# One reordering on ScalarE and a new split of 48 small sums in a fused long-convolution and cosine-gated MLP kernel on one Trainium2 core

## The chip, the cores and the metric

The kernel runs on one core of a Trainium2 chip (trn2). A core has five engines that run their own instruction streams in order and wait for each other by semaphores: PE (TensorE, matrix products), DVE (VectorE), ACT (ScalarE), POOL (GpSimd), and SP (SyncE), which here only issues DMAs. The metric is the device time of one execution in microseconds (us); less is better. Before the change it is 3781.08 us, the median of 6 runs between 3780.34 and 3785.08.

## What is computed

A long convolution per channel (as in Hyena), and an MLP with a cosine gate on its rows:

```
h_filt = (maximum(pos_emb @ w1, 0) @ w2) * exp(-0.01 * pos)    # one filter of length 12480 per channel
u      = x * v                                                 # 4 x 12480 x 128
y      = causal convolution of u with h_filt along the sequence (by FFT of length 2*S)
rows   = (x * y).reshape(49920, 128)
h      = rows @ w_in                                           # 49920 x 2048
out    = (h * cos(h)) @ w_out                                  # 49920 x 128
```

## The kernel before, in words

**The convolution** is done by two-step transforms written as small matrix products: a first and a second forward step (`f1`, `f2`; the product with the filter's transform is in `f2`), and a first and second inverse step (`i1`, `i2`). They run batch by batch, b = 0 to 3. The second inverse step works on 30 groups of `G` = 4 columns of the sequence. For each group it needs four matrices of 96 x 2 x 104 numbers, the tile `tm`. For b = 0 most of them are made on the spot by `make_group` (line 642), which calls `make_t` and that calls `turn` (line 284) once for each matrix; the group is then stored to DRAM (`td`, line 651) and later batches load it from there (line 670). Six of the 30 groups (2, 7, 12, 17, 22 and 27, `SOME`) are made earlier, beside `i1` of batch 0, by `some_groups`; those are loaded by b = 0 too.

A matrix is the sum of two scaled terms. Two forms of it exist in `turn`: ACT writes the first term into `tm` (line 291) and DVE scales and adds the second in one instruction (line 293); or ACT writes the first term into `tm` (line 291) and the second into a spare tile (line 296), and POOL adds the two (line 297). In a group of b = 0, matrices 0 and 1 take the first form and matrices 2 and 3 the second, with one spare buffer. In `some_groups` all four take the second form, with two.

**The MLP** runs over 98 tiles of up to 128 rows of four columns each (`BANK` = 512 numbers per partition), and each tile over 16 chunks of 128 hidden units. One chunk of one tile is a step. In step i:

- PE multiplies into a bank `ph` (`moe_up`, line 737). Four banks exist, and the transposes of a tile (`moe_turn`, `moe_back`, line 126) take theirs from the same four.
- ACT scales and shifts `ph` into `a` (line 740), DVE finds the whole turns `k` (line 743), POOL subtracts them, `f` (line 746).
- One step later (`moe_act`) ACT takes the Sin of `f` (`cs`, line 751) and DVE multiplies by `ph` to the gate `gt` (line 753), which frees that bank `ph`.
- `LAG` = 4 steps later PE multiplies `gt` into the accumulator of the tile (`moe_down`, line 762). After a tile's last chunk ACT copies the sums out (`moe_evict`, `ot`, line 768), and they are transposed back and stored later.

The accumulator has one bank (`ps_acc`, tile `acc`), so that the first `moe_down` of a tile waits for the `ot` of the tile before. Once the last convolution group has been issued, every other tile takes a bank of the convolutions instead (`cv` in place of `acc` on line 762).

**The order** is written by hand (`manual_schedule`): what the Python loop issues first stands first in each engine's queue. The loop over `steps` at the end issues `moe_up` of step i, `moe_act` of step i - 1, `moe_down` of step i - 4 and, after a tile's last chunk, `moe_evict`. In the same step as `moe_evict`, `moe_turn` of a later tile follows (PE transposes and the ACT copy `at`, line 731). Then the loop draws convolution work: each `yield` of the generators gives its cost in steps, and work is drawn until what is owed is paid. A group of `i2` with b = 0 costs 3.5 steps in four parts. In part p the generator issues the p-th matrix of the next group (`units`, the iterator `early`), the products of the current group in parts 0 and 2, and between them `inverse_units` draws the loading and multiplying of the next batch's input (`u_units`: `xt`, line 392, and the sums `slots` of line 398), in which the first half of every other multiplication is on POOL and all others on DVE.

Of the kernel before, what the change touches and what calls it, by code (L numbers as in the profile page):

```python
# [9 lines left out]
F32 = mybir.dt.float32  # L10
# [20 lines left out]
def kernel(  # L31
# [51 lines left out]
    N1, N2 = 96, 120  # L83
    R = S // N2
# [15 lines left out]
    G = BANK // D  # L100
# [204 lines left out]
    def make_t(t, n2, **how):  # L305


        i = 1 if n2 < H - 1 else 0
        turn(t, rows[:, i:i + 2, :], rows[:, i + 1:i + 3, :], tw_t[:, 0, n2:n2 + 1],
             tw_t[:, 1, n2:n2 + 1], **how)  # L310
# [54 lines left out]
    def n2s(g):  # L365

        a = g * UA
        return [*range(a, a + UA), *range(N2 - UA - a, N2 - a)]
# [270 lines left out]
            yield from units(CB, I1_STEPS, lambda j: None, mm,  # L639
                             lambda j, ps: i1_evict(pool, ps, j), 2)  # L640

    def make_group(pool, g, t, summed, bufs=1):

        for i, n2 in enumerate(n2s(g)):
            if i < G - summed:
                make_t(t[:, i, :, :], n2)
            else:
                spare = pool.tile([N1, 2, R], F32, name="spare", bufs=bufs)
                make_t(t[:, i, :, :], n2, spare=spare[:, :, :])
            yield  # L650
        nc.sync.dma_start(td[g, :, :, :, :], t[:, :, :, :])

    def some_groups(pool):
        for g in SOME:
            t = pool.tile([N1, G, 2, R], F32, name="some", bufs=2)
            yield from make_group(pool, g, t, G, bufs=2)
        next(backs[0])

    def i2_units(bank, b, bufs):

        with tc.tile_pool(name="back", bufs=2, side="left" if b else "right") as pool:
            ts, xss = {}, {}

            def before(j):
                ts[j] = pool.tile([N1, G, 2, R], F32, name="tm", bufs=bufs)
                xss[j] = pool.tile([R, 2, UA * D], F32, name="xs", bufs=bufs)
                load_pairs(xss[j], x, b, n2s(j)[0], n2s(j)[UA])
                if b == 0 and j not in SOME:
                    return make_group(pool, j, ts[j], G // 2)
                nc.sync.dma_start(ts[j][:, :, :, :], td[j, :, :, :, :])  # L670

            def mm(j, ps, i):
                if i == 0:
                    ps = bank()
                i2_mm(ps, ts[j], j, i)
                return ps

            yield from units(NG, I2_STEPS, before, mm,
                             lambda j, ps: i2_out(pool, ps, xss.pop(j), b, j),
                             4 if b == 0 else 2, ahead=bufs - 1)  # L680
# [34 lines left out]
    def rows_of(n):  # L715
        return first_row(n + 1) - first_row(n)
# [7 lines left out]
    def moe_turn(pool, n):  # L724
        m = rows_of(n)
        zb = zbs.pop(n)
        pt = ps_h.tile([P, BANK], F32, name="ph")
        for i in range(G):
            transpose(pt[:, i * m:(i + 1) * m], zb[0:m, i, :], ident)
        at = pool.tile([D, BANK], F32, name="at")  # L730
        nc.scalar.copy(out=at[:, 0:G * m], in_=pt[:, 0:G * m])
        ats[n] = at

    def moe_up(pool, n, c):
        m = G * rows_of(n)
        ph = ps_h.tile([P, BANK], F32, name="ph")
        nc.tensor.matmul(ph[:, 0:m], w_in_sb[:, c * P:(c + 1) * P], ats[n][:, 0:m],  # L737
                         start=True, stop=True)
        a = pool.tile([P, BANK], F32, name="a", bufs=3)
        nc.scalar.activation(a[:, 0:m], ph[:, 0:m], AF.Identity,  # L740
                             bias=quarter[:, 0:1], scale=INV_TWO_PI)
        k = pool.tile([P, BANK], F32, name="k")
        nc.vector.tensor_scalar(out=k[:, 0:m], in0=a[:, 0:m], scalar1=ROUND,  # L743
                                scalar2=ROUND, op0=ALU.add, op1=ALU.subtract)
        f = pool.tile([P, BANK], F32, name="f")
        nc.gpsimd.tensor_tensor(f[:, 0:m], a[:, 0:m], k[:, 0:m], op=ALU.subtract)  # L746
        return ph, f, m

    def moe_act(pool, ph, f, m):
        cs = pool.tile([P, BANK], F32, name="cs")  # L750
        nc.scalar.activation(cs[:, 0:m], f[:, 0:m], AF.Sin, scale=TWO_PI)  # L751
        gt = pool.tile([P, BANK], F32, name="gt", bufs=4)
        nc.vector.tensor_tensor(gt[:, 0:m], ph[:, 0:m], cs[:, 0:m], op=ALU.mult)  # L753
        return gt

    def moe_down(n, c, gt):
        if c == 0:

            accs[n] = bank() if made[0] == B * NG and n % 2 else \
                ps_acc.tile([P, BANK], F32, name="acc")  # L760
        m = G * rows_of(n)
        nc.tensor.matmul(accs[n][:, 0:m], w_out_sb[:, c, :], gt[:, 0:m],  # L762
                         start=(c == 0), stop=(c == NFC - 1))

    def moe_evict(pool, n):
        m = G * rows_of(n)
        ot = pool.tile([D, BANK], F32, name="ot", bufs=1)
        nc.scalar.copy(out=ot[:, 0:m], in_=accs.pop(n)[:, 0:m])  # L768
        return ot

    def moe_back(pool, n, ot):
        m = rows_of(n)
        pt = ps_h.tile([P, BANK], F32, name="ph")
        for i in range(G):
            transpose(pt[0:m, i * D:(i + 1) * D], ot[:, i * m:(i + 1) * m], ident)
        ob = pool.tile([P, 2, UA * D], F32, name="ob", bufs=1)
        nc.scalar.copy(out=ob[0:m, :, :].rearrange("p h n -> p (h n)"), in_=pt[0:m, :])
        return ob

    def moe_store(n, ob):  # L780
        row = first_row(n)
        while row < first_row(n + 1):
            b, g, n1 = row // R // NG, row // R % NG, row % R
            count = min(R - n1, first_row(n + 1) - row)
            first, _, second, _ = n2s(g)
            start = out[b * S + n1 * N2 + first, :]
            at = row - first_row(n)
            nc.sync.dma_start(
                bass.AP(tensor=start.tensor, offset=start.offset,
                        ap=[[N2 * D, count], [(second - first) * D, 2], [1, UA * D]]),  # L790
                ob[at:at + count, :, :])
            row += count

    with tc.manual_schedule():
        with tc.tile_pool(name="psum", bufs=8, space=PSUM) as psum, \
# [103 lines left out]
            nc.vector.memset(quarter[:, :], 0.25)  # L899
            nc.sync.dma_start(w_in_sb[:, :], wind[:, :])  # L900
            beside(i1_units(bank), [(w_out_sb[:, c, :], w) for c, w in out_pieces], some_groups)

        ps_acc = ctx.enter_context(tc.tile_pool(name="ps_acc", bufs=1, space=PSUM))
        ps_h = ctx.enter_context(tc.tile_pool(name="ps_h", bufs=4, space=PSUM))
        ps_c = ctx.enter_context(tc.tile_pool(name="ps_c", bufs=3, space=PSUM))
        mpool = ctx.enter_context(tc.tile_pool(name="moe", bufs=2))
# [14 lines left out]
        def load(n):  # L921
            while made[0] * R < first_row(n + 1):
                next(conv)
            moe_load(mpool, n)
# [4 lines left out]
        steps = [(n, c) for n in range(NALL) for c in range(NFC)]  # L929
        hidden, gates, ots, obs = {}, {}, {}, {}  # L930
        for i in range(len(steps) + LAG):
            if i < len(steps):
                n, c = steps[i]
                if n == 0 and c == NFC // 2:
                    load(1)
                if c == NFC - 4 and n + 2 < NALL:
                    load(n + 2)
                hidden[i] = moe_up(mpool, n, c)
            if 0 <= i - 1 < len(steps):
                gates[i - 1] = moe_act(mpool, *hidden.pop(i - 1))  # L940
            if i >= LAG:
                pn, pc = steps[i - LAG]
                moe_down(pn, pc, gates.pop(i - LAG))
                if pc == NFC - 1:
                    ots[pn] = moe_evict(mpool, pn)
            if i < len(steps):

                if c == (LAG - 1 if n else NFC - 2) and n + 1 < NALL:
                    moe_turn(mpool, n + 1)
                if c == NFC // 2 and n - 1 in ots:  # L950
                    obs[n - 1] = moe_back(mpool, n - 1, ots.pop(n - 1))
                if c == NFC // 2 + 2 and n - 1 in obs:
                    moe_store(n - 1, obs.pop(n - 1))
            owed += 1.0
            while owed > 0.0:
                owed -= next(conv, owed)
# [30 lines left out]
```

## Time and profile before

One execution was profiled. Its time was 3780.34 us; its span, from the first to the last instruction, is 3778.6 us.

| what | busy us (share of the span) | instructions |
|---|---|---|
| PE | 3699.7 (98%) | 13546 |
| DVE | 2761.6 (73%) | 5562 |
| POOL | 2591.5 (69%) | 2342 |
| ACT | 2519.0 (67%) | 4683 |
| time of the profiled execution | 3780.34 | |
| median of the 6 runs | 3781.08 | |

Stretches of the span: up to 337 us the filter, the tables and the transforms of batch 0; 337 to 580 us `i2` of batch 0, with the first MLP tiles beside it; 580 to 3000 us the other batches beside the MLP; from 3000 us the MLP alone.

How to read the views: a group line gives the source line, engine, operation, output <- inputs, how often, busy us and mean ns. A line of the view of waits reads "engine line <- releaser: us in total, times, longest us". A line of the timeline gives start, duration, engine, line, operation and tiles, "x2" where two neighbours are merged; a product of 512 columns in float32 is two matmul records, which start 0.43 us apart and are recorded as 0.59 us each, because they are pipelined. PEld is the loading of a product's stationary operand, and an idle time of 0.24 us before one is the usual spacing. In brackets stands the idle time before the instruction and what ended it.

### The profile page before, as it was taken

How to read it: one execution, taken by the hardware profiler on the slowest of the kernel's cores; microseconds unless marked ns; L12 is line 12 of the kernel's file. 1: busy time of each engine (PE TensorE's matmuls, PEld its weight loads, DVE VectorE, ACT ScalarE, POOL GpSimd, SP SyncE). 2: the span in 40 equal slices, each digit the busy share in tenths (PEclk: the TensorE clock that was granted, in tenths of full speed). 3: DMA queues.
4: the chain of work that ended last, by engine and by line, in shares of the span. 5: the costliest groups of instructions: out<-in, count | busy, mean ns of one | idle time of the engine just before them, and what ended most of it. 6: DMA issues, size and time to landing. Idle time of an engine off the chain costs nothing.

```text
span 3778.6 us, 47199 instructions
## 1 busy us (share of the span) xinstructions
PE 3699.7 (98%) x13546; PEld 2107.4 (56%) x13546; DVE 2761.6 (73%) x5562; ACT 2519.0 (67%) x4683; POOL 2591.5 (69%) x2342
## 2 busy tenths in 40 slices
PE   8898999999999999999999999999999999999999
PEld 6777555655466555555565556555566544444444
DVE  7887887688766777778766786788765566666666
ACT  5757776766665557766655567666664677777777
POOL 7667886588854665688745664788644577777776
PEclk9999999999999999999999999999999999999999
DMA  6263441022202650122103540122105200000000
GB/s 166 67 181 108 149 148 54 19 72 77 74 18 69 182 155 27 35 76 79 57 18 111 176 123 21 48 79 75 41 12 169 86 22 18 17 21 19 17 22 13
DMA packets 209498, 276.14 MB, mean 73 GB/s; under 512 B 17111, under 2 KB 146535, under 8 KB 209111
## 3 DMA queue, kind: packets, MB, share of 16 engines
q1 hardware_dynamic: 209239, 273.12, 24.3%
q8 instruction: 109, 1.79, 0.2%
q14 instruction: 150, 1.23, 0.1%
HBM read 193.64 MB, written 79.42 MB: 72 GB/s over the span
## 4 chain that ended last, share of the span: by engine, by line
PE 85%; POOL 6%; DVE 3%; ACT 2%; DMA 2%; issue 2%; SPq 0%; POOLq 0%; DVEq 0%; ACTq 0%
PE ph L737 32%; PE acc L762 27%; PE cv L762 5%; PE cv L501 5%; PE cv L476 4%; POOL f L746 3%; PE cv L404 3%; PE cv L445 3%; PE ph L126 2%; PE ps L445 1%; PE ps L404 1%; PE ps L476 1%; DVE k L743 1%; POOL tm L297 1%; ACT cs L751 1%
## 5 line engine op out<-in xcount | busy, mean ns | idle before, releaser
L746 POOL TENSOR_TENSOR f<-a,k 128x512 f32<-128x512 f32 (+1 forms) x1568 | 1985.5, 1266 | 1049.7 <-DVE k L743 1048.7
L737 PE MATMUL ph<-at,w_in_sb 128*128 128x512 f32 (+1 forms) x3136 | 1598.9, 591 | 6.0 <-DVE gt L753 5.4
L740 ACT ACTIVATE a<-ph,quarter 128x512 f32<-128x512 f32 (+1 forms) x1568 | 1072.5, 684 | 758.8 <-PE ph L737 749.0
L762 PE MATMUL acc<-gt,w_out_sb 128*128 128x512 f32 (+1 forms) x2688 | 1374.3, 593 | 9.4 <-ACT ot L768 9.1
L753 DVE TENSOR_TENSOR gt<-ph,cs 128x512 f32<-128x512 f32 (+1 forms) x1568 | 1076.9, 687 | 317.2 <-ACT cs L751 289.1
L743 DVE TENSOR_SCALAR k<-a 128x512 f32<-128x512 f32 (+1 forms) x1568 | 768.7, 490 | 620.6 <-ACT a L740 604.0
L751 ACT ACTIVATE cs<-f 128x512 f32<-128x512 f32 (+1 forms) x1568 | 980.5, 625 | 328.9 <-POOL f L746 326.6
L762 PEld LDWEIGHTS acc<-gt,w_out_sb 128*128 128x128 f32 x2688 | 505.6, 189 | 662.2 <-issue 619.3
L737 PEld LDWEIGHTS ph<-at,w_in_sb 128*128 128x128 f32 x3136 | 553.6, 190 | 338.6 <-issue 269.1
L471 POOL TENSOR_TENSOR slots<-slots,t 120x256 f32<-120x256 f32 x384 | 311.5, 817 | 58.8 <-DVE t L464 36.2
L501 PEld LDWEIGHTS cv<-slots,tm 96*104 96x104 f32 x1920 | 239.9, 170 | 108.4 <-issue 80.9
L501 PE MATMUL cv<-slots,tm 96*104 96x128 f32 x1920 | 253.5, 274 | 9.7 <-DVE tm L293 4.9
L762 PE MATMUL cv<-gt,w_out_sb 128*128 128x512 f32 (+1 forms) x448 | 224.5, 583 | 0.7 <-DVE gt L753 0.7
L476 PEld LDWEIGHTS cv<-cs,slots 120*96 120x96 f32 x1536 | 176.7, 167 | 67.6 <-issue 65.7
L476 PE MATMUL cv<-cs,slots 120*96 120x120 f32 x1536 | 183.1, 266 | 0.0
L445 PE MATMUL cv<-slots,w 124*120 124x256 f32 x576 | 173.0, 380 | 0.0
L445 PEld LDWEIGHTS cv<-slots,w 124*120 124x120 f32 x576 | 103.6, 184 | 123.8 <-issue 110.9
L404 PEld LDWEIGHTS cv<-c,slots 104*124 104x124 f32 x768 | 132.5, 192 | 71.2 <-issue 58.3
L404 PE MATMUL cv<-c,slots 104*124 104x192 f32 x768 | 151.2, 326 | 4.7 <-DVE gt L753 3.4
L762 PEld LDWEIGHTS cv<-gt,w_out_sb 128*128 128x128 f32 x448 | 84.9, 190 | 104.5 <-issue 99.5
L392 DVE TENSOR_TENSOR xt<-xt,vt 104x256 f32<-104x256 f32 x177 | 137.8, 786 | 0.0
L486 DVE TENSOR_TENSOR slots<-cv,other 96x240 f32<-96x240 f32 x384 | 133.7, 394 | 4.2 <-ACT other L484 4.2
(129 smaller groups left out, 2567.0 us busy)
## 6 DMA issues: line engine op xcount, KB each, us to landing
h<-hd SPq DMA_DIRECT2D x144, 240.0 KB
tm<-td SPq DMA_DIRECT2D x96, 312.0 KB
xt<-in_x_dram SPq DMA_DIRECT2D x120, 208.0 KB
vt<-in_v_dram SPq DMA_DIRECT2D x120, 208.0 KB
xs<-in_x_dram SPq DMA_DIRECT2D x120, 208.0 KB
zd<-zs SPq DMA_DIRECT2D x119, 208.0 KB
zb<-zd SPq DMA_DIRECT2D x96, 256.0 KB
w<-wd SPq DMA_DIRECT2D x144, 116.2 KB
```

Of the source, the lines that this page charges most:

```text
L404: nc.tensor.matmul(ps[0:KE, i * 2 * N1:(i + 1) * 2 * N1], u[:, b, 0:KE, i], c1[0:u.shape[0], :, :].rearrange("p r k -> p (r k)"), start=Tr ...
L445: nc.tensor.matmul(pi, w[:, i, :], parts[0:KE, :, k], start=True, stop=True)
L471: nc.gpsimd.tensor_tensor(y[:, r], y[:, r], t[:, r], op=op)
L476: nc.tensor.matmul(ps[0:N1, (i * 2 + r) * N2:(i * 2 + r + 1) * N2], parts[0:N2, r, :, b, i], cs[:, r, :], start=True, stop=True)
L501: nc.tensor.matmul(ps[0:R, i * D:(i + 1) * D], t[:, i, r, :], slots[0:N1, :, place, :], start=(r == 0), stop=(r == 1))
L737: nc.tensor.matmul(ph[:, 0:m], w_in_sb[:, c * P:(c + 1) * P], ats[n][:, 0:m], start=True, stop=True)
L740: nc.scalar.activation(a[:, 0:m], ph[:, 0:m], AF.Identity, bias=quarter[:, 0:1], scale=INV_TWO_PI)
L743: nc.vector.tensor_scalar(out=k[:, 0:m], in0=a[:, 0:m], scalar1=ROUND, scalar2=ROUND, op0=ALU.add, op1=ALU.subtract)
L746: nc.gpsimd.tensor_tensor(f[:, 0:m], a[:, 0:m], k[:, 0:m], op=ALU.subtract)
L751: nc.scalar.activation(cs[:, 0:m], f[:, 0:m], AF.Sin, scale=TWO_PI)
L753: nc.vector.tensor_tensor(gt[:, 0:m], ph[:, 0:m], cs[:, 0:m], op=ALU.mult)
L762: nc.tensor.matmul(accs[n][:, 0:m], w_out_sb[:, c, :], gt[:, 0:m], start=(c == 0), stop=(c == NFC - 1))
```

## The change

Two edits. In the groups of b = 0, DVE now makes matrices 0 and 2 and POOL matrices 1 and 3, and the spare tile has two buffers. `some_groups` still gives all four to POOL, with two buffers. In the loop over steps, `moe_down` of step i - 4 and the `moe_evict` behind it are issued ahead of `moe_act` of step i - 1. Since PE has no instruction in `moe_act` and ACT and DVE have none in `moe_down`, this changes the order of one engine alone: on ACT, once a tile, the copy `ot` stands ahead of the Sin of step i - 1 in place of behind it.

```diff
-    def make_group(pool, g, t, summed, bufs=1):
+    def make_group(pool, g, t, summed):
 
         for i, n2 in enumerate(n2s(g)):
-            if i < G - summed:
+            if summed < G and i % 2 == 0:
                 make_t(t[:, i, :, :], n2)
             else:
-                spare = pool.tile([N1, 2, R], F32, name="spare", bufs=bufs)
+                spare = pool.tile([N1, 2, R], F32, name="spare", bufs=2)
                 make_t(t[:, i, :, :], n2, spare=spare[:, :, :])
             yield
         nc.sync.dma_start(td[g, :, :, :, :], t[:, :, :, :])
...
-            yield from make_group(pool, g, t, G, bufs=2)
+            yield from make_group(pool, g, t, G)
...
                 hidden[i] = moe_up(mpool, n, c)
-            if 0 <= i - 1 < len(steps):
-                gates[i - 1] = moe_act(mpool, *hidden.pop(i - 1))
             if i >= LAG:
                 pn, pc = steps[i - LAG]
                 moe_down(pn, pc, gates.pop(i - LAG))
                 if pc == NFC - 1:
                     ots[pn] = moe_evict(mpool, pn)
+            if 0 <= i - 1 < len(steps):
+                gates[i - 1] = moe_act(mpool, *hidden.pop(i - 1))
```

## The prediction

> **What bounds the kernel now.** I read the page's busy times and its chain, then the view of waits, then stretches by window, then the timeline around the ends of tiles.
>
> ```profile
> PE 3699.7 (98%) x13546; PEld 2107.4 (56%) x13546; DVE 2761.6 (73%) x5562; ACT 2519.0 (67%) x4683; POOL 2591.5 (69%) x2342
> PE 85%; POOL 6%; DVE 3%; ACT 2%; DMA 2%; issue 2%; SPq 0%; POOLq 0%; DVEq 0%; ACTq 0%
> ```
>
> PE is the bound: 98% busy, 85% of the chain. So an edit on other engines is worth only what it takes from, or adds to, PE's waits. The waits that the edits touch:
>
> ```profile
> ACT cs L751 <- POOL f L746: 326.6, 882, 2.9
> PEld acc L762 <- ACT ot L768: 39.9, 45, 2.3
> PE acc L762 <- ACT ot L768: 9.1, 15, 1.5
> ACT spare L296 <- POOL tm L297: 7.2, 12, 0.7
> ```
>
> After a tile's end the first product of the next tile waits for `ot`, which stands on ACT behind a Sin that itself waits for `f`. The windows (PE, PEld, DVE, ACT, POOL busy, then the granted clock):
>
> ```profile
> 337.00:580.00 243.00, 231.15 (x919) 134.19 (x920) 201.97 (x337) 177.51 (x355) 203.88 (x185) 0.98 0.51 153
> 385.00:389.00 4.00, 3.49 (x11) 2.44 (x12) 3.06 (x7) 2.39 (x6) 3.13 (x3) 0.60 0.23 58
> 3000.00:3779.00 779.00, 773.35 (x1982) 355.64 (x1980) 493.57 (x881) 604.40 (x963) 553.81 (x440) 1.00 0.07 19
> ```
>
> Edit one acts only in 337 to 580 us, where POOL (84%) and DVE (83%) are nearly as full as PE (95%).
>
> **Edit two, `ot` ahead of the Sin.** A tile's end in the middle stretch, between two steps:
>
> ```profile
> 1629.04 1.02 PE L762 MATMUL acc<-gt,w_out_sb 128*128 128x512 f32 x2
> ...
> 1629.51 1.28 POOL L746 TENSOR_TENSOR f<-a,k 128x512 f32<-128x512 f32 x1
> ...
> 1630.77 1.02 PE L737 MATMUL ph<-at,w_in_sb 128*128 128x512 f32 x2
> 1630.82 0.63 ACT L751 ACTIVATE cs<-f 128x512 f32<-128x512 f32 x1 [0.90 <-POOL f L746]
> ...
> 1631.36 0.57 ACT L768 COPY ot<-acc 128x512 f32<-128x512 f32 x1
> ...
> 1631.98 1.12 PE L762 MATMUL acc<-gt,w_out_sb 128*128 128x512 f32 x2 [0.18 <-ACT ot L768]
> ...
> 1632.94 1.02 PE L737 MATMUL ph<-at,w_in_sb 128*128 128x512 f32 x2
> ```
>
> The last sums are ready at 1630.06 (1629.04 + 1.02), ACT is idle until `f` ends at 1630.79, and `ot` starts at 1631.36. PE's product should start at 1630.77 + 2 x 0.43 = 1631.63; it starts at 1631.98, 0.35 late, and its second half 0.10 later still (the next product is 0.96 behind it in place of 0.86): 0.45 us lost. Afterwards `ot` runs from about 1630.11 to 1630.68, inside ACT's idle time: the loss goes, and the Sin isn't late. The idle column alone understates this (0.18 here), as a record lasts 0.59 and its successor could start after 0.43. So I added up, from the start times at all 98 ends, start minus the natural start, and the 0.10. From 600 to 3000 us that gives 10.05 us at 26 tiles: 0.52 at 617, 2.73 at six tiles from 841 to 1043, 2.21 at seven from 1565 to 1766, 2.14 at six from 2418 to 2585, 1.73 at 2687 and 0.72 at five others. With `ot` at the end of the last product or of the preceding `a`, whichever is later, plus 0.05, every one of them is gone.
>
> What is behind the moved copy on ACT: this Sin, `at`, conversions of convolution banks, the next `a`. Where the Sin was ready it becomes 0.44 to 0.75 us late (0.46 from the start of `ot` to the next instruction, plus ACT's wait for the last product). Its `gt` is late with it, and late next is the `moe_up` two steps on, which takes the bank that this `gt` frees. With the Sin's new time I redid that wait for each tile: 0.80 us come back, at 1407, 1565, 2687 and in traces at four others. The convolution's banks hide the rest: 0.87 us (2262) to 1.3 us are left there before the next use, above 0.75. `td` stores, PE's and SP's queues keep their order. I take 10.05 - 0.80 = 9.25, less 0.75 for waits that return a few steps later: 8.5. Bounds: 4, the idle row alone (9.1, of which 4.2 lie before 580 and 0.8 at 584), and 10.
>
> The end, from 3000 us, has nothing to win (accumulators alternate), and the least cover:
>
> ```profile
> 3414.85 1.02 PE L762 MATMUL acc<-gt,w_out_sb 128*128 128x512 f32 x2
> ...
> 3415.93 0.63 ACT L751 ACTIVATE cs<-f 128x512 f32<-128x512 f32 x1 [0.19 <-POOL f L746]
> ...
> 3416.47 0.57 ACT L768 COPY ot<-acc 128x512 f32<-128x512 f32 x1
> ...
> 3416.60 0.69 DVE L753 TENSOR_TENSOR gt<-ph,cs 128x512 f32<-128x512 f32 x1 [0.33 <-ACT cs L751]
> ...
> 3417.44 0.19 PEld L737 LDWEIGHTS ph<-at,w_in_sb 128*128 128x128 f32 x1 [0.24 <-DVE gt L753]
> ```
>
> `ot` will start at 3415.91 (3414.85 + 1.02 + 0.04), the Sin at 3416.37, 0.44 late; `gt` ends at 3417.73 in place of 3417.29, and the load can start 0.05 later, 3417.78, 0.34 late. Over the trace, loads that start up to 0.32 us after the preceding product cost nothing, and from 0.43 on the excess plus 0.10. So 0.02 us a tile x 27 = 0.6. If the Sin were 0.75 late as elsewhere, the load would be 0.65 late: 0.22 + 0.10 = 0.33, x 27 = 8.8. I take 0.6, since these 27 ends are alike to 0.01 us. Bounds 0 and 8.8.
>
> In 337 to 580 us (six ends, the last at 584) the same sum gives 5.55 us gone and 1.84 back. But here `f` falls behind PE within every tile, from 2.6 us after its product to 6, and PE's stalls at the end are what lets it catch up; without them the next ends wait more for `gt`. I take half of 3.7: 1.8 (bounds 0, 3.7). Two ends there, 385 and 505, are followed by a granted clock of 0.60 and 0.57 for 4 us, 1.6 + 1.7 us of PE; with shorter stalls they may go: 1.0 (bounds 0, 3.3).
>
> The Trainium skill (TensorE: Matmul & The Clock Gate, HAM oscillation) asks for idle gaps over some 3.4 us before the clock falls; by that, shorter stalls here save none of this. No gap in front of these two is that long in the trace, so the trace differs, and the 1.0 stands by the windows.
>
> **Edit one.** 24 groups, 48 matrices each way, before and after: no work is added. Instruction order of both kernels: PE and SP the same. In half of the groups parts 1 and 2 fall in one MLP step, and POOL's order doesn't change at all; in the others its first sum moves ahead of `xt`, out of the part in which DVE multiplies. Rows from the timelines of POOL and ACT:
>
> ```profile
> 531.09 1.77 POOL L297 TENSOR_TENSOR tm<-tm,spare 96x208 f32<-96x208 f32 x1
> ```
> ```profile
> 532.89 0.47 ACT L296 ACTIVATE spare<-rows,tw_t 96x208 f32<-96x208 f32 x1 [0.74 <-POOL tm L297]
> ```
>
> The second row goes with two buffers: 7.2 us of ACT in all, and the `a` behind it comes sooner; POOL's next `f` was then late by 0.35, x 10 of the 12 such waits = 3.5. The first: POOL's first sum of a group takes 1.28 on the mean, its second 0.76, and 0.62 alone. In the changed groups it should fall to about 0.9: 0.4 x 11 = 4.4 of POOL. Against that, POOL gets `f`, a sum and `xt` (1.27 + 0.9 + 1.0) in one step of 2.2 us. Of 7.9 I take 3 on PE. Bounds: +8 (all of it), and -12 (11 groups in which `xt` of 1.1 delays `f` on the chain).
>
> The Trainium skill (Perfetto Trace Analysis, Optimizing Scalar/DVE Operations) speaks against this edit: POOL and DVE share a read port that one instruction locks, so that moving work between them may not help. The 1.77 row agrees with such a lock; by the rule alone the 3 would be 0 and the time 3770.4.
>
> **Sum:** 8.5 + 1.8 + 1.0 + 3.0 - 0.6 = 13.7 us. The profiled execution (span 3778.6, 1.7 around it) took 3780.34, 0.7 under the median; from the median, 3781.08 - 13.7 = 3767.4.
>
> **Rivals.**
> 1. *Batch 0's stretch gives all back*: POOL's rate sets it, and edit one leaves it. For: `f` lags there through each tile. Against: POOL is idle 39 of 243 us. 3781.1 - 8.5 + 0.6 = 3773.2.
> 2. *Slower: POOL's step with two extra operations.* In 337 to 580 us, `f` behind sum and `xt` delays Sin and `gt`, and PE stalls at tile ends for the bank `ph`. Price 12 as above plus four more clock drops at 1.65 = 18.6: 3773.2 + 18.6 = 3791.8. Beyond 7.9 the change is slower, beyond 15.4 by over 0.2%. For: PE waits there for `gt` 3.9 us even now. Against: the next step has no sum, and four steps of lag smooth it.
> 3. *The late Sin costs at the end* 8.8 rather than 0.6: 3767.4 + 8.2 = 3775.6. For: PE's ends are modelled. Against: `a` follows a modelled end by 0.04 throughout.
> 4. *Edit one doesn't do what it says* in half the groups is counted above.
>
> **Chances.** Forecast 0.55 (own range 3761 to 3773), rival 1 0.20, rival 2 0.11, rival 3 0.14. Within 0.2%, 7.6 us, a measurement of this kernel can't tell it from none: that is 3773.5 to 3788.6. Faster: 0.51 + half of rival 1 = 0.61. Slower: 0.10 of rival 2. Same: the rest, 0.29. Rival 3, rival 1 and the bounds of batch 0's stretch put the upper end at 3781; the lower is 3757: the forecast less the rest of the bounds (1.5 + 1.9 + 2.3 + 5 = 10.7).
>
> **What would show it.** Right: `acc` waiting for `ot` nearly gone between 600 and 3000 us; Sin later by 0.4 at tile ends after 3000 with PE's 773 us unchanged; 12 waits of `spare` gone; the stretch 337 to 580 shorter by some 6. Wrong: PE waiting for `gt` where it waited for `ot`, a longer stretch after 3000, more clock drops before 580.

## The result and the profile after

| kernel | median us (lowest to highest, runs) | ratio to before (95% interval) |
|---|---|---|
| before | 3781.97 (3779.14 to 3786.94, 36) | |
| after | 3771.77 (3769.3 to 3775.1, 16) | 0.9973 (0.9966 to 0.9979) |

The change makes the kernel 10.2 us faster. The execution that was profiled took 3775.76 us (span 3774.0), 4.0 above the median of after, and that of before 1.6 below the median of the table. So a comparison of these two traces shows 4.6 us (3778.6 - 3774.0) of the 10.2, and a difference of 2 or 3 us between two single executions proves little. Where it matters I use several kernels' traces.

The page of after, busy times and the chain's shares by engine:

```profile
PE 3695.9 (98%) x13546; PEld 2108.8 (56%) x13546; DVE 2778.6 (74%) x5562; ACT 2517.6 (67%) x4683; POOL 2569.0 (68%) x2342
PE 86%; DVE 4%; DMA 3%; POOL 3%; ACT 2%; issue 2%; SPq 0%; POOLq 0%; DVEq 0%; ACTq 0%
```

PE is the bound as before. POOL lost 22.5 us of work and DVE gained 17.0, though both do the same operations as before: each count is unchanged. The waits of the whole execution that answer to those shown of before:

```profile
ACT cs L751 <- POOL f L746: 384.1, 877, 2.9
...
PEld ph L737 <- ACT at L731: 16.7, 41, 0.8
...
ACT ot L768 <- PE acc L762: 11.4, 66, 0.3
...
PEld cv L501 <- DMA tm<-td: 10.8, 12, 3.3
```

`ot` now waits for the last sums (at most 0.3 us), as the diff intends, where before it waited behind a Sin. For 583 to 2995 us, the same view of after:

```profile
PEld acc L762 <- ACT ot L768: 5.9, 24, 0.4
...
PEld cv L501 <- DMA tm<-td: 4.9, 7, 1.3
...
PE cv L501 <- DMA tm<-td: 3.4, 4, 1.2
```

Before, the first of these lines read 31.6 us, 40 times, up to 2.3, and there was a second, of PE itself, with 4.9 us; that one is gone. What is left of the first is 24 waits of 0.25 on the mean (0.4 at most), about the usual spacing of 0.24. The two lines of `tm` grew: they were 2.9 and 2.3. The timeline at the end of a tile, the same tile as shown of before:

```profile
1629.36 1.02 PE L762 MATMUL acc<-gt,w_out_sb 128*128 128x512 f32 x2
...
1629.82 1.28 POOL L746 TENSOR_TENSOR f<-a,k 128x512 f32<-128x512 f32 x1
...
1630.42 0.58 ACT L768 COPY ot<-acc 128x512 f32<-128x512 f32 x1 [0.17 <-PE acc L762]
...
1631.10 1.02 PE L737 MATMUL ph<-at,w_in_sb 128*128 128x512 f32 x2
1631.13 0.63 ACT L751 ACTIVATE cs<-f 128x512 f32<-128x512 f32 x1
...
1631.95 1.02 PE L762 MATMUL acc<-gt,w_out_sb 128*128 128x512 f32 x2
```

`ot` starts 0.04 us after the sums (1630.38), while `f` still runs, and the Sin follows `f` (1631.10) by 0.03. The next `moe_down` starts 0.85 us after its `moe_up`, the undisturbed distance (2 x 0.43); before it was 1.21. This is what the prediction described for PE and for `ot`.

Two stretches by window (PE, PEld, DVE, ACT, POOL busy, then the granted clock), and one that follows a long wait:

```profile
337.00:583.00 246.00, 232.10 (x921) 134.09 (x922) 211.10 (x341) 176.30 (x359) 183.77 (x187) 0.98 0.51 152
...
431.00:435.00 4.00, 4.00 (x9) 1.76 (x8) 2.65 (x6) 1.92 (x4) 1.91 (x3) 0.59 0.47 138
2995.00:3774.00 779.00, 773.62 (x1984) 355.74 (x1982) 492.52 (x881) 604.95 (x963) 553.83 (x440) 1.00 0.07 19
```

In the first, before had 204.97 of DVE and 205.57 of POOL in a window of the same length: 6.1 us more and 21.8 less. The second shows that a drop of the clock remains, at another place; it follows this piece of the chain (start, us, what):

```profile
424.19 0.92 PE ph L737 x2
425.11 5.15 DMA tm<-td
430.25 0.04 issue
430.30 1.13 PE cv L501 x8
```

PE waits at 430 for the matrices of a group that is loaded, not made. To place the gains, I cut each trace at events that all kernels have: the first convolution product of batch 0's inverse, and the ends of tiles 5, 69 and 95 (in before at 337, 581, 2991 and 3728 us). Times are in us, each stretch from one trace; the ratios come from timed runs, each against before in its own session. The medians of before were 3782.0 beside after, 3784.7 beside e1 to e4, 3784.6 beside e5 to e8 and 3785.9 beside e9 and e10, so that ratios and not medians are to be compared.

| kernel | batch 0, to tile 5 | tiles 5 to 69 | tiles 69 to 95 | median | ratio (95% interval) |
|---|---|---|---|---|---|
| before | 243.7 | 2409.5 | 737.16 | | |
| after | 244.8 | 2402.8 | 736.97 | 3771.8 | 0.9973 (0.9966 to 0.9979) |
| e1 `ot` first, no turns | 242.7 | 2405.8 | 736.97 | 3774.4 | 0.9975 (0.9966 to 0.9985) |
| e2 turns only | 244.6 | 2411.3 | 737.16 | 3784.4 | 1.0000 (0.9991 to 1.0009) |
| e3 second spare only | 243.7 | 2414.6 | 737.16 | 3782.8 | 0.9999 (0.9990 to 1.0008) |
| e4 after, `tm` load first | 242.3 | 2398.4 | 736.97 | 3768.4 | 0.9963 (0.9949 to 0.9976) |
| e5 after, `moe_turn` first too | 245.0 | 2406.5 | 736.97 | 3778.9 | 0.9985 (0.9976 to 0.9994) |
| e6 `ot` and load first, no turns | 242.6 | 2399.4 | 736.97 | 3767.9 | 0.9956 (0.9943 to 0.9968) |
| e7 after, all matrices by DVE | 240.1 | 2403.5 | 736.97 | 3769.4 | 0.9957 (0.9942 to 0.9973) |
| e8 after, all by POOL | 249.5 | 2403.7 | 736.97 | 3781.7 | 0.9995 (0.9986 to 1.0004) |
| e9 e6, all by DVE | 236.4 | 2399.6 | 736.97 | 3763.9 | 0.9940 (0.9927 to 0.9954) |
| e10 e7, ACT's copies kept | 238.6 | 2405.9 | 736.97 | 3767.9 | 0.9955 (0.9941 to 0.9969) |

### The profile page after: what moved, and what is told of

It is laid out like the page before. It is cut to its first block, busy times and chain, and to the rows that moved or that the text cites. A ratio compares the mean times of both kernels' runs of the same rounds, so it can differ in the third digit from the quotient of the medians.

```text
span 3774.0 us, 47191 instructions
## 1 busy us (share of the span) xinstructions
PE 3695.9 (98%) x13546; PEld 2108.8 (56%) x13546; DVE 2778.6 (74%) x5562; ACT 2517.6 (67%) x4683; POOL 2569.0 (68%) x2342
## 4 chain that ended last, share of the span: by engine, by line
PE 86%; DVE 4%; DMA 3%; POOL 3%; ACT 2%; issue 2%; SPq 0%; POOLq 0%; DVEq 0%; ACTq 0%
PE ph L737 33%; PE acc L762 28%; PE cv L762 5%; PE cv L501 5%; PE cv L476 4%; PE cv L445 3%; PE cv L404 3%; PE ph L126 2%; POOL f L746 2%; DMA hd<-h 2%; PE ps L404 1%; DMA tm<-td 1%; PE ps L476 1%; ACT cs L751 1%; DVE gt L753 1%
## 5 line engine op out<-in xcount | busy, mean ns | idle before, releaser
L743 DVE TENSOR_SCALAR k<-a 128x512 f32<-128x512 f32 (+1 forms) x1568 | 796.4, 508 | 549.9 <-ACT a L740 537.7
```

## The experiments

**e1, e2, e3: the two edits, and the second spare buffer, each alone.** e1 is before with only this:

```diff
-            if 0 <= i - 1 < len(steps):
-                gates[i - 1] = moe_act(mpool, *hidden.pop(i - 1))
             if i >= LAG:
...
+            if 0 <= i - 1 < len(steps):
+                gates[i - 1] = moe_act(mpool, *hidden.pop(i - 1))
```

> Edit two alone: the copy of a tile's sums ahead of the Sin, the groups of batch 0 as before. Theory A (the prediction's terms): 8.5 us gained between 580 and 3000 us, 2.8 in batch 0's stretch with the clock drops, 0.6 lost after 3000: about 10.7 us faster, ratio 0.9972. Theory B (the stretch of batch 0 gives everything back, because there the vector engines and the loads set the pace): 8.5 - 0.6 = about 8 us faster, 0.9979, and 337 to 581 us as long as before. In both, no wait of acc for ot in the profile from 580 us on, and the Sin at a tile's end 0.4 to 0.75 us late.

e2 is before with the other edit, to `make_group` and its call in `some_groups`, as the change has it:

```diff
-            if i < G - summed:
+            if summed < G and i % 2 == 0:
...
-                spare = pool.tile([N1, 2, R], F32, name="spare", bufs=bufs)
+                spare = pool.tile([N1, 2, R], F32, name="spare", bufs=2)
```

> Edit one alone: matrices by DVE and POOL by turns and two spare buffers, the Sin ahead of the sums' copy as before. Theory A: POOL's sums in batch 0's stretch take about 0.77 us on the mean instead of 1.02, and 3 us of it reach PE: 3778 to 3779, ratio 0.9992. Theory B: POOL's time is saved (48.9 to some 37 us) but PE waits instead for the loads of the six groups that were made earlier, so no gain: 1.0000 plus or minus 0.0005.

e3 is before with a second buffer and no turns:

```diff
-                    return make_group(pool, j, ts[j], G // 2)
+                    return make_group(pool, j, ts[j], G // 2, bufs=2)
```

> Only the second spare buffer of edit one; matrices 0 and 1 by DVE, 2 and 3 by POOL as before, the Sin first as before. Every engine's order is that of before. Theory A: the 12 waits of ACT's spare for POOL's sum (7.2 us) go and some 2 us reach PE: 0.9995. Theory B: the waits go, and nothing reaches PE: 1.0000. If POOL's sums keep their mean of 1.02 us here, the shorter sums of the changed kernel come from the turns and not from the buffer.

Measured: 0.9975 for e1, 1.0000 for e2, 0.9999 for e3. The whole gain is that of the copy's place; the turns and the buffer bring nothing (to 0.1%). In e3 the 12 waits of `spare` for POOL's sum (7.2 us) are gone, and nothing of them reaches PE. What the turns do is seen in three groups of 337 to 583 us, first of before (the last numbers are busy us, mean ns, and the idle time ahead):

```profile
L746 POOL TENSOR_TENSOR f<-a,k 128x512 f32<-128x512 f32 x83 | 105.3, 1269 | 27.5 <-DVE k L743 27.5
...
L297 POOL TENSOR_TENSOR tm<-tm,spare 96x208 f32<-96x208 f32 x48 | 48.9, 1019 | 2.5 <-ACT spare L296 2.5
L743 DVE TENSOR_SCALAR k<-a 128x512 f32<-128x512 f32 x84 | 43.5, 517 | 21.7 <-ACT a L740 21.7
```

The same groups of after:

```profile
L746 POOL TENSOR_TENSOR f<-a,k 128x512 f32<-128x512 f32 x82 | 104.0, 1269 | 47.4 <-DVE k L743 46.4 <-PE ph L737 1.0
...
L743 DVE TENSOR_SCALAR k<-a 128x512 f32<-128x512 f32 x83 | 51.6, 622 | 10.4 <-ACT a L740 9.7 <-POOL f L746 0.7
...
L297 POOL TENSOR_TENSOR tm<-tm,spare 96x208 f32<-96x208 f32 x48 | 37.2, 774 | 1.4 <-ACT spare L296 1.2
```

POOL's sums fell from 1.019 to 0.774 us each, 11.7 us in all, more than the 4.4 forecast. But DVE's `k` rose from 0.517 to 0.622 (8.7 us over 83 of them), and `k` stands ahead of every `f`. What POOL saved in all, 21.8 us, became waiting: its idle time ahead of `f` grew by 19.9. In e3 the sums stay at 1.021, so it is the turns and not the buffer that shorten them; `k` is at 0.564 there, so that nearly half of its rise comes with the second buffer alone. My reading is that the blocked time went from a POOL operation that had some slack to a DVE operation ahead of it; that `k` passes it on to PE is not shown by itself.

**e4 and e6: the load of the matrices ahead of the load of the input.** The chain above waits for `tm<-td`. In the code that load stands on SP behind the load of `xs` (`load_pairs`), which waits until DVE's `zs` of an earlier group has read the buffer that it fills (0.8 us at this group). e4 is after with:

```diff
+                made_here = b == 0 and j not in SOME
+                if not made_here:
+                    nc.sync.dma_start(ts[j][:, :, :, :], td[j, :, :, :, :])
                 load_pairs(xss[j], x, b, n2s(j)[0], n2s(j)[UA])
-                if b == 0 and j not in SOME:
+                if made_here:
                     return make_group(pool, j, ts[j], G // 2)
-                nc.sync.dma_start(ts[j][:, :, :, :], td[j, :, :, :, :])
```

> The changed kernel, and in the second inverse step the load of a group's matrices is issued ahead of the load of x on SP's queue, so that it no longer stands behind a transfer that waits for DVE's product of two groups before. Theory B (the stretch's gain goes into these waits): PE's waits for tm from DRAM (3.8 us before 583, 3.4 later, in the profile of the changed kernel) fall below 2 us in all, and the time is 3 to 6 us under the changed kernel: about 3767, ratio to before 0.996. Theory A (they are a matter of single runs): the time is that of the changed kernel within 1.5 us, 0.9973.

e6 has the same edit and the copy's place, and matrices 0 and 1 by DVE and 2 and 3 by POOL as in before. Unlike what its expectation says, it keeps the second spare buffer, as after does.

> Edit two and the load of a group's matrices ahead of the load of x, without edit one (matrices 0 and 1 by DVE, 2 and 3 by POOL, one spare buffer). If edit one is worth nothing or costs up to 1 us, as its run alone showed: 0.9962 plus or minus 0.0006, as with it (0.9963), or 1 us better. If edit one's saving on POOL was only held back by the loads and shows once these are early: 3 us slower than with it, 0.9971.

SP's timeline at the load of the group that stalled at 430, in after:

```profile
423.47 0.33 SPq L651 DMA_DIRECT2D td<-tm  x1
424.69 0.31 SPq L373 DMA_DIRECT2D xs<-in_x_dram  x1
425.11 0.34 SPq L670 DMA_DIRECT2D tm<-td  x1
```

and in e4:

```profile
423.01 0.33 SPq L651 DMA_DIRECT2D td<-tm  x1
423.44 0.37 SPq L669 DMA_DIRECT2D tm<-td  x1
424.24 0.33 SPq L373 DMA_DIRECT2D xs<-in_x_dram  x1
```

The load starts 0.43 us after the store ahead of it, in place of 1.64. In e4 no wait of PE's products for `tm<-td` remains, in e6 1.1 us of it, where after has 3.8 (to 583 us) and 3.4 (behind that). Tiles 5 to 69 are 5.2 us shorter than without the edit (mean of e4, e6 and e9, 2399.1, against 2404.4 for after, e1, e7, e8 and e10; the two sets don't overlap). So a load came last at some places where PE no longer waited for `ot`. How much of the 5.2 us the early load would have given with the Sin first is open: no run has that. e6 against e1, both without turns (e6 with the second buffer): 0.9956 against 0.9975, whose intervals still overlap; the traces are the clearer evidence. e6 is no slower than e4 (0.9963), so that edit one's saving was not merely held back by the loads.

**e5: a later Sin still.** e5 is after with the transposes of the next tile, and so the copy `at`, also ahead of the Sin:

```diff
+            if i < len(steps):
+                if c == (LAG - 1 if n else NFC - 2) and n + 1 < NALL:
+                    moe_turn(mpool, n + 1)
             if 0 <= i - 1 < len(steps):
...
-                if c == (LAG - 1 if n else NFC - 2) and n + 1 < NALL:
-                    moe_turn(mpool, n + 1)
```

> The changed kernel with the transposes of the next tile and their copy at issued ahead of the Sin as well, so that the Sin of a tile's end is late by two copies (0.92 us) in place of one. The prediction's rule (a load of weights up to 0.32 us late costs nothing, from 0.43 on the excess plus 0.10): after 3000 us the load is 0.80 late at each of 27 ends, 0.37 + 0.10 = 0.47 a tile, 12.5 us; between 600 and 3000 us 3.2 us more than in the changed kernel; about 15.7 us slower than the changed kernel, ratio to before 1.0015. Rival (a late Sin is made up for elsewhere, the four steps of lag hide it): the time of the changed kernel, 0.9973, and the 27 tiles after 3000 us as long as before (737.2 us between the last products of tiles 69 and 95).

Measured: 0.9985, 736.97 us for tiles 69 to 95, the same as in after to 0.01 us, though the Sin is later by one more copy. A tile's end there in e5:

```profile
3385.80 0.64 ACT L751 ACTIVATE cs<-f 128x512 f32<-128x512 f32 x1
...
3386.37 0.19 PEld L737 LDWEIGHTS ph<-at,w_in_sb 128*128 128x128 f32 x1 [0.24 <-issue]
3386.47 0.69 DVE L753 TENSOR_TENSOR gt<-ph,cs 128x512 f32<-128x512 f32 x1 [1.27 <-ACT cs L751]
3386.79 1.02 PE L737 MATMUL ph<-at,w_in_sb 128*128 128x512 f32 x2
```

The load of the second `moe_up` behind the tile's end begins 0.10 us before this `gt` has even begun, and its product starts 0.37 us before `gt` ends (3387.16). It does not take the bank that this `gt` frees. In after the same load, at 3412.75, names its releaser:

```profile
3411.59 0.63 ACT L751 ACTIVATE cs<-f 128x512 f32<-128x512 f32 x1
...
3412.12 0.57 ACT L731 COPY at<-ph 128x512 f32<-128x512 f32 x1
...
3412.25 0.69 DVE L753 TENSOR_TENSOR gt<-ph,cs 128x512 f32<-128x512 f32 x1 [0.79 <-ACT cs L751]
...
3412.75 0.51 PEld L737 LDWEIGHTS ph<-at,w_in_sb 128*128 128x128 f32 x2 [0.35 <-ACT at L731]
```

It starts when the copy `at` has ended (3412.69) and before `gt` has (3412.94): it takes the bank of the transposes. In before it is the other way round. There the same load (3417.44, shown in the prediction) names `gt`, which ended at 3417.29, and it starts before `at` has ended (3417.52):

```profile
3416.93 0.59 ACT L731 COPY at<-ph 128x512 f32<-128x512 f32 x1
```

The waits behind 2995 us say the same of all tiles there, first of before, then of after:

```profile
PEld ph L737 <- DVE gt L753: 13.2, 55, 0.3
```
```profile
PEld ph L737 <- ACT at L731: 9.1, 26, 0.4
PEld ph L737 <- DVE gt L753: 7.2, 29, 0.4
```

26 of the 55 went from `gt` to `at`, one for each tile's end. The line of after with 26 waits for `at` stands in every trace with `ot` first except e5's, where `at` comes earlier; before, e2 and e3 have none. So the edit changed more than ACT's order: with the copy ahead of the Sin, the four banks `ph` are taken in another order, and the late `gt` frees the one that the third `moe_up` takes. That load has time to spare even in e5: it starts at 3388.08, 0.92 us after this `gt`. By the ratios e5 is 4.5 us slower than after (0.0012 x 3782; the intervals just overlap). Its trace doesn't say where: it is 3.7 us longer than that of after over tiles 5 to 69, in small parts without a wait that carries it, and no longer than those of e1 and e10 by more than 1 us. That stays open.

**e7, e8, e10: who makes the matrices.** e1 to e3 say that the turns win nothing; another split might. e7 is after with no matrix of batch 0's groups on POOL, e8 with all on POOL:

```diff
-            if summed < G and i % 2 == 0:
+            if i < G - summed:
...
-                    return make_group(pool, j, ts[j], G // 2)
+                    return make_group(pool, j, ts[j], 0)
```

```diff
-                    return make_group(pool, j, ts[j], G // 2)
+                    return make_group(pool, j, ts[j], G)
```

> The changed kernel with all four matrices of a group of batch 0 made by DVE, none by POOL. If POOL's rate sets the stretch of batch 0 (37 us of sums go from it): several us faster than the changed kernel, 0.9955. If DVE, or the port that both share, sets it as much as POOL: DVE gets 48 more instructions of 0.5 to 0.9 us, k behind them comes later, and the stretch of 245 us grows by 5 to 20 us: 0.999 to 1.003.

> The changed kernel with all four matrices of a group of batch 0 made by POOL, none by DVE. If DVE's rate sets the stretch: faster than the changed kernel by several us, 0.9955. If POOL's does: 48 more sums of 0.8 us and 48 more terms on ACT of 0.45 us, the stretch grows by 15 to 35 us: 1.001 to 1.006. If both this and all by DVE are slower, neither engine alone sets the stretch, and moving sums between them has nothing to win.

Measured: 0.9957 and 0.9995, and 240.1 and 249.5 us for batch 0's stretch, where after has 244.8. So the split matters after all: the intervals of e7 and e8 lie apart. `k` in e7, then in e8, in 337 to 583 us:

```profile
L743 DVE TENSOR_SCALAR k<-a 128x512 f32<-128x512 f32 x85 | 40.2, 472 | 4.7 <-ACT a L740 4.5
```
```profile
L743 DVE TENSOR_SCALAR k<-a 128x512 f32<-128x512 f32 x81 | 59.9, 740 | 13.1 <-ACT a L740 11.7 <-POOL f L746 0.7
```

With `ot` first, and the load where after has it, the stretch goes with the length of `k`: 0.472 (e7) 240.1, 0.515 (e1) 242.7, 0.622 (after) 244.8, 0.740 (e8) 249.5. POOL's sums change along with `k` in these four, so that the runs don't tell the two apart. In e7 DVE does 48 more terms and is 92% busy (226.4 of 246), and the stretch is still the shortest of these four: the busy share of DVE does not set it. In e8 PE also waits 9.1 us for POOL's sums. But e7 takes two things away, POOL's sums and 48 copies `spare` of ACT (22 us). e10 puts the copies back, into buffers that nothing reads:

```diff
                 make_t(t[:, i, :, :], n2)
+                if i % 2:
+                    spare = pool.tile([N1, 2, R], F32, name="spare", bufs=2)
+                    row = 1 if n2 < H - 1 else 0
+                    nc.scalar.activation(spare[:, :, :], rows[:, row + 1:row + 3, :], AF.Copy,
+                                         scale=tw_t[:, 1, n2:n2 + 1])
```

> e7 (all matrices of batch 0's groups by ACT and DVE) with the 48 scaled copies on ACT that POOL's sums needed still made, into two spare buffers that nothing reads. It is work added that the output doesn't use. It tells POOL's share of e7's gain from ACT's. Theory 'POOL's sums set that stretch': it stays at 240 to 241 us, 0.9957 of before. Rival 'ACT's copies set it' (22 us of ACT came off in e7): it goes back to 242.7 to 245 us, where e1 and the kernel after are, 0.9965 to 0.9975 of before.

Measured: 0.9955 and 238.6 us; `k` takes 0.477. The copies on ACT cost nothing, and e7's gain comes from POOL's sums having gone. e10's stretch is even 1.5 shorter than e7's; that difference lies where the clock stayed low for longer in e7, in 431 to 435 us (0.57, in e10 0.92).

**e9: the parts that helped, together.** e6 with no matrix of batch 0's groups on POOL.

> e6 (the sums' copy ahead of the Sin, the matrices' load ahead of that of the input) with all 96 matrices of batch 0's groups in the form of ACT and DVE, none on POOL. If the gains are of different places they add: e7's stretch of batch 0 was 240.07 us against 242.64 in e6, its later stretches those of the kernel after, and e6's later stretches 3 us shorter than that. Theory 'they add': 3767.9 - 2.6 = 3765.3 us, 0.9950 of before (0.9943 to 0.9957), stretch of batch 0 at 239 to 241 us. Rival 'both take the same waits for the matrices' (the waits of products for loaded or made matrices move from one to the other): 0.9956 as e6, stretch near 242.5 us.

Measured: 3763.89 us, 0.9940 (0.9927 to 0.9954), the fastest of all medians, 22 us under before in the same session (3785.86). Its stretch of batch 0, 236.4 us, is 6.2 shorter than e6's where 2.6 was expected. Part of this is the clock: in e6 it was 0.56 from 341 to 349 us, and the 33rd product of the stretch starts 11.6 us after the first, where in e9 (0.82) and e4 (0.92) it is 9.0. Without these 2.5 us 3.7 are left. The trace of e9 shows no drop of the clock between 345 and 3750 us, as e4 doesn't.

## Why the prediction was right, and where it was wrong

**Right: what edit two removes.** Every wait of PE for `ot` behind 583 us is gone, with `ot` where the arithmetic put it. The term of 8.5 for tiles behind 580 us: the two traces give 6.7 (2409.5 - 2402.8); the mean of the five kernels with `ot` first and the old load order against before, e2 and e3 gives 7.4 (2411.8 - 2404.4). It lay within its bounds, 4 and 10.

**Wrong: "late next is the `moe_up` two steps on, which takes the bank that this `gt` frees".** That was read rightly off the trace of before, and it holds there. The prediction took it over to after, but the edit itself changes the order of the banks: in after this load waits for `at`. So the 0.80 that was to come back, the 0.6 lost at the end and rival 3 had no path. Tiles 69 to 95 became 0.19 us shorter, not 0.6 longer, and Sin's lateness is free there even with one more copy ahead of it. As far as the prediction goes this is luck, since nothing in it foresaw the new order; what a Sin this late would cost in the old one no run shows.

**Wrong: what takes back.** The allowance of 0.75 "for waits that return a few steps later" named no place. A place that the traces show is the load of `tm`, 1.1 us more of PE's waits behind 583 us (3.4 for 2.3) and 2.4 more before it (3.8 for 1.4), and with the load moved ahead the middle stretch gains 12.7 in place of 7.4 against the kernels with the old order of `ot`. This wait was visible in the trace of before, as 2.3 us.

**Wrong: "Of 7.9 I take 3 on PE", edit one.** e2 puts it at 0 (1.0000, 0.9991 to 1.0009, or -3.4 to +3.4 us), and the stretch it acts in is 0.9 longer in e2 than in before and 2.1 longer in after than in e1; e4's is 0.4 shorter than e6's, but e6's holds the 2.5 us of its clock. So in the traces the turns cost some 1 to 2 us, which the timed runs can't resolve. Neither part of the 7.9 reached PE: e3 has the waits of `spare` gone and gains nothing, and the shorter sums went with a longer `k`. The saving on POOL was there, and larger; that DVE's `k` would grow with it was not counted, though the prediction had the rule that says so beside it and set it aside. The Trainium skill (SBUF — State Buffer, Who interferes with whom) says that where an instruction of VectorE needs the port pair that it shares with GpSimd, the one that issues first holds the pair for its whole length, and that the order decides who is blocked. The rows fit this: with the sums moved in the order, the sums fell by 0.245 us each and `k` rose by 0.105; which instructions hold the pair no row shows.

**Half right: batch 0's stretch, 1.8 + 1.0.** `ot` first alone gives 1.0 us there (242.7 in e1 for 243.7 in before), clock included. The two drops at 386 and 505 went, but one came at 430 in e1 and 431 in after, behind the wait for `tm`. One drop less, at the prediction's 1.6 to 1.7 us, is more than that 1.0. By this estimate the term of 1.8 for the copy's place gave nothing, and the 1.0 for the clock came out with two drops gone and a new one made, which is luck. In after, with edit one, the stretch is 1.1 us longer than in before, not some 6 shorter. Nothing of rival 2's size appeared: no `f` delayed the stretch by anything near 12 us. Rival 1's sum, 3773.2, is nearer to the measured 3771.8 than the forecast, 3767.4: its outcome for that stretch, all given back, is what after shows, though its reason (that POOL's rate sets it and edit one leaves it) is only half of it, since edit one shortened POOL's work and the stretch didn't follow, while with POOL's sums gone (e7, e10) it did.

**The sum.** 7.4 + 1.0 + 0 + 0.2 = 8.6 us from the traces, where 13.7 was forecast; the timed runs give 10.2, from 7.9 to 12.9 by the interval of the ratio. The gain is 3.5 us short of the forecast. The terms that gave nothing, edit one's 3.0 and the copy's 1.8 in batch 0's stretch, are more than that.

## What to carry to other kernels

When an operation is taken out of another's way, follow both engines that run beside each other: a saving on GpSimd can turn up as a longer instruction on VectorE. In these traces the stretch went with the length of the instruction on the chain (here `k`, ahead of `f`, Sin and `gt`), and not with the busy share of either engine. When a wait of PE is removed, look at once for the next thing that PE waits for in the same stretch, here a load queued on SP behind another load that waits for a buffer; moving it ahead made the middle stretch 5.2 us shorter, half of what the change itself gave. And an edit that only moves one instruction in one engine's order can change which buffer each tile gets, and with it what waits for what: a path that was read off the trace of before has to be looked for again in that of after.

## What the runs showed of the hardware

- The same operation on the same shape takes very different times by what runs beside it: `k` 0.472 us on the mean with no sums on POOL, 0.740 with 96 of them; `xt` on DVE 0.510 and 1.179 in the same two kernels. Taking the sums from POOL and giving them to a DVE that was 86% busy (211.1 of 246 us in after, 226.4 in e7) made the stretch 4.7 us shorter.
- The clock fell to 0.59 in 431 to 435 us behind a gap of 2.44 us between PE's products. The Trainium skill (TensorE: Matmul & The Clock Gate, HAM oscillation) gives as the rule that PE have no idle gaps over about 3.4 us; this trace shows a drop behind a shorter one. e1, e7, e8 and e10, with the load where after has it, have one that starts between 427 and 431 us too (e5, also with that load, has one at 515 in its place); e4, e6 and e9, in which the load comes earlier, show none there.
